# Forty more zero products on the tensor engine, and row sums in four buffers, in an attention and two-MLP kernel

## The chip, the cores and the metric

The kernel runs on one core of a Trainium2 chip. The metric is the device time of one execution in microseconds (us). Before the change three timed executions took 489.66, 491.88 and 491.96 us, a median of 491.88 us.

## What is computed

Two batches, eight heads, 768 positions, 64 columns a head, all in float32. The attention is banded: a position sees itself, the 95 before it and 8 global ones, with a bias by distance. Two mixing layers follow it. Cut to what matters:

```
scores = scale * q @ k.T + bias;  scores = where(keep, scores, -1e9)
a = exp(scores - max(scores));  a = a / (sum(a) + 1e-9);  x = a @ v
u = x + (relu(x.T @ w_tok1) @ w_tok2).T
x = u + relu(u @ w_ch1) @ w_ch2
h = relu(x @ w_in);  u, v = halves of h;  v = (v - mean) / sqrt(var + 1e-6)
out = (u * (w_spatial @ v + b_spatial)) @ w_out
```

## The kernel before

**Stages.** The first 110 us or so hold attention; the rest is dense products, where each float32 product is made of three (lines 333 to 335, `mm3`: high by high, low by high, high by low part). Attention is cut into 12 groups of two units for two heads each. For a group TensorE makes the scores (line 461), VectorE adds the bias and takes the row's extreme into `nm` (486), ScalarE takes exp in place in tile `e` with the row sums into `rs` (490), TensorE transposes `e` (496), ScalarE copies the result to `pt` (338), TensorE multiplies with v (522) and transposes back (532), and VectorE divides by the row sums (541, 542, 547). Beside it ScalarE and VectorE turn 64-bit weights into two float32 parts (379 to 386, the staging tile `raw` of pool `stgp`), and TensorE makes the first token products of a half batch (lines 333 to 335, `p<-xh,wth`, in PSUM banks 6 and 7) and the second ones (711 and `p<-wth,hh`).

**What sets the order.** Every step is an `Op` with a list of engines it may run on and an estimated cost. `Plan.run` is a list scheduler: at each step it takes, of the operations that could start first by its estimates, the one with the longest chain of work behind it, and appends its instructions to their engine's queue. The order in each engine's queue is therefore fixed when the program is built. On the chip an engine does its queue in order and waits for semaphores.

**Zero products.** `banded_part` adds `IDLE[0]` products of a tile of zeros into PSUM bank 7 (line 566, 256 columns, bf16), of which nothing is read. The i-th may not be placed before 4.0 + 0.2 i us of the planner's time. Each waits only for the one before it; the first user of bank 7 after them is the second half (f = 1) of the first token products, so all of them stand before that. They are placed where the planner has no other work for TensorE that could start as early, or where their chain is longer than that of the work that could.

**Row sums.** `rs` is a tile of 32 bytes a partition with 3 rotating buffers, in pool `att`, which is filled from one end of SBUF. In the built program `raw`, `bias0`, `bias1` and `e` of that pool begin 32 bytes past a multiple of 64 (`raw` at 172,448), while `pt`, `ct` and `xp`, and the tile `first` that serves as the first `raw`, begin at multiples of 64. The two `raw` buffers of `stgp` are 4,128 bytes long and begin at 83,776 (a multiple of 64) and 87,904 (32 past one).

Of the kernel before, what the change touches and what calls it, by code (L numbers as in the profile page):

```python
# [6 lines left out]
F32 = mybir.dt.float32  # L7
# [9 lines left out]
P = 128  # L17
# [26 lines left out]
RB, OB = (2, 3), (0, 1, 4, 5, 6, 7)  # L44

WARM = 9
IDLE = 40, 4.0, 0.2

SWITCH, TURN = 0.16, 2.0
_OUTS = [((B, S, DM), "float32")]  # L50
# [36 lines left out]
class Plan:  # L87
# [13 lines left out]
    def op(self, where, fn, reads=(), writes=(), pri=None, mode="full"):  # L101
        o = Op(where, fn, self.pri if pri is None else pri, len(self.ops))
        o.mode = mode if where[0][0] == "PE" else None
        o.plan, o.lam = self, self.lam
        for key in reads:
            w, r = self.seen.setdefault(key, [[], []])
            o.deps.update(w)
            r.append(o)
            if isinstance(key[0], Buf):
                key[0].users.append(o)  # L110
        for key in writes:
            w, r = self.seen.setdefault(key, [[], []])
            o.deps.update(r)
            o.deps.update(w)
            self.seen[key] = [[o], []]
            if isinstance(key[0], Buf):
                key[0].users.append(o)
                if key[0].first is None:
                    key[0].first = o
        o.deps.discard(o)  # L120
        self.ops.append(o)
        return o
# [64 lines left out]
def act(n, extra=0.0):  # L187
    return ("ACT", n / 1200 + 0.07 + extra)


def dve(n, x=1):
    return ("DVE", n * 0.00104 / x + 0.07)
# [10 lines left out]
def mm(n, count):  # L203
    return ("PE", count * (max(n, 64) / 2400 + 0.003))
# [70 lines left out]
class Arm:  # L275
# [227 lines left out]
    def group(self, units):  # L503

        op, T, V = self.plan.op, self.T, self.V
        banks = self.scores(units)
        rs = self.buf("att", "rs", [P, 2, 2, 2, 1], F32, 3)  # L510
        pts = [[self.unit(b, 2 * hp + i, u, banks[k][i], rs, k) for i in range(2)] for k, (b, hp, u) in enumerate(units)]
        c = self.bank("c", CB)

        def pv(e):
            for k, (b, hp, u) in enumerate(units):
                v = self.raws[b, hp]()[:, QK:].rearrange("p (t h x) -> p t h x", h=2, x=D)
                for t, o, w in self.tiles(u):
                    blocks = [(o, t)] if t == 0 else [(o, NT + t - 1), (o + P, t)]
                    sl = slice((2 * k + t % 2) * P, (2 * k + t % 2 + 1) * P)
                    for z, (o1, i) in enumerate(blocks):  # L520
                        for h in range(2):
                            T.matmul(c()[h * D:h * D + D, sl], lhsT=v[:, i, h], rhs=pts[k][h]()[:, o1:o1 + P],  # L522
                                     start=(z == 0), stop=(z == len(blocks) - 1))

        op([("PE", sum(3 if u == 0 else 4 for _, _, u in units) * 0.22)], pv,
           [(p,) for x in pts for p in x] + [self.rawk[b, hp] or ("raw0", "v") for b, hp, _ in units], [(c,)], mode="columns")
        ct = self.buf("att", "ct", [P, 512], F32, 1)
        op([act(512), dve(512)], lambda e: self.copy(e, ct(), c()), [(c,)], [(ct,)])

        def back(e):  # L530
            for j in range(4):
                T.transpose(c()[:, j * P:(j + 1) * P], ct()[:, j * P:(j + 1) * P], self.ident)  # L532

        op([("PE", 0.44)], back, [(ct,)], [(c,)])
        for b, hp, u in units:
            if u == 0:
                self.x_at(b, hp)
                if hp % 2 == 0:
                    self.x_alloc(b, hp // 2)
        rks = [(rs, k, j, i) for k in range(2) for j in range(2) for i in range(2)]  # L540
        op([("DVE", 0.08)], lambda e: V.tensor_scalar(out=rs(), in0=rs(), scalar1=1e-9, scalar2=None, op0=ALU.add), [], rks)
        op([("DVE", 0.11)], lambda e: V.reciprocal(rs(), rs()), [], rks)
        for k0, k1 in ((0, 2),) if units[0][1] == units[1][1] else ((0, 1), (1, 2)):
            b, hp, u = units[k0]
            xp, ks = self.xp[b, hp]
            n = 2 * (k1 - k0)
            op([dve(2 * n * D)], lambda e, xp=xp, u=u, n=n, k0=k0, k1=k1: V.tensor_tensor(
                out=xp()[:, 2 * u:2 * u + n].rearrange("p t (h d) -> p t h d", d=D),
                in0=c()[:, 256 * k0:256 * k1].rearrange("p (t h d) -> p t h d", h=2, d=D),
                in1=rs()[:, k0:k1].rearrange("p k t h o -> p (k t) h o").to_broadcast([P, n, 2, D]), op=ALU.mult),  # L550
                [(c,)] + rks, ks[u:u + k1 - k0] + ([("raw0", x) for x in "abv"] if (b, hp) == (0, 1) else []))
        for b, hp, u in units:
            if u == 2:
                self.plan.pri = XP
                self.x_done(b, hp)
                self.plan.pri = 0.0

    def banded_part(self):
# [5 lines left out]
        idle = self.bank("p7", (7,))  # L564
        for i in range(IDLE[0]):
            o = plan.op([mm(256, 1)], lambda e: self.T.matmul(  # L566
                idle()[:, :256], lhsT=self.zero, rhs=self.zero[:, 0:1].broadcast_to([P, 256]), start=True, stop=True), [], [(idle,)], 9.0)
            o.ready = IDLE[1] + i * IDLE[2]
        self.bias = {}
# [428 lines left out]
```

## Time and profile before

| | |
|---|---|
| median of three timed executions | 491.88 us (489.66 to 491.96) |
| the profiled execution | 489.34 us, span 487.6 us |
| PE busy | 479.2 us (98%) |
| DVE, ACT, POOL busy | 295.9, 215.7, 43.9 us |
| zero products | 40, the last one begins at 32.3 us |

PE stands for TensorE, DVE for VectorE, ACT for ScalarE, POOL for GpSimd, SP for the queue that issues the DMAs. Times are from the span's start. A matmul's end is modelled and overlaps the next one, so a short wait of PE hides inside its busy time: it is read from the start of one group of matmuls to the start of the next, or from a group that is longer than the same group elsewhere.

### The profile page before, as it was taken

Reading aid. Unit: us, or ns where it says so; the run is one execution under the profiler, and the core shown is the slowest. Engines: PE = TensorE matmul, PEld = TensorE weight load, DVE = VectorE, ACT = ScalarE, POOL = GpSimd, SP = SyncE. Lnnn points to the kernel's source line nnn. Section 1 sums busy time; section 2 is a strip of 40 time slices with the busy share of each in tenths; the row PEclk is TensorE's granted clock in tenths of the full one; section 3 lists DMA queues with packets and bytes.
Section 4 is the critical chain, followed back from the end, with each engine's and each line's share of the span. In section 5 each row is a group of like instructions: output and inputs, shape, how many; then the busy total and the mean of one; then the engine's idle time right before and its main releaser. Section 6 shows DMA issues by size and latency. Waiting matters only on the chain.

```text
span 487.6 us, 7897 instructions
## 1 busy us (share of the span) xinstructions
PE 479.2 (98%) x3037; PEld 418.9 (86%) x3037; DVE 295.9 (61%) x747; ACT 215.7 (44%) x518; POOL 43.9 (9%) x36
## 2 busy tenths in 40 slices
PE   9999999999999999999989999999999999999996
PEld 5778678989998888888878888988899988899985
DVE  5779988998988986202888772335861511721520
ACT  5999998995655454211233321103422112421111
POOL 0131311111000000000500000003330000000000
PEclk9999999999999999999999999999999999999999
DMA  7645637222343434000023421110000011000012
GB/s 286 248 169 165 253 91 271 104 84 101 123 144 118 165 105 156 0 1 0 1 86 100 153 72 32 40 59 0 1 1 1 0 65 66 1 2 0 1 43 93
DMA packets 10989, 41.48 MB, mean 85 GB/s; under 512 B 1344, under 2 KB 1856, under 8 KB 10048
## 3 DMA queue, kind: packets, MB, share of 16 engines
q1 hardware_dynamic: 10944, 40.90, 23.7%
q8 instruction: 26, 0.43, 0.4%
q14 instruction: 19, 0.16, 0.1%
HBM read 37.75 MB, written 3.15 MB: 84 GB/s over the span
## 4 chain that ended last, share of the span: by engine, by line
PE 87%; DVE 9%; ACT 1%; issue 1%; POOL 1%; DVEq 0%; POOLq 0%; ACTq 0%
PE p L333 24%; PE p L335 24%; PE p L334 24%; PE p L461 4%; PE p L496 3%; PE p L522 3%; DVE first L344 2%; DVE e L486 1%; DVE uy0l L344 1%; PE p L566 1%; PE p L532 1%; PE dummy L248 1%; PE p L711 1%; DVE a L386 1%; DVE raw L344 1%
## 5 line engine op out<-in xcount | busy, mean ns | idle before, releaser
L758 ACT ACTIVATE raw<-p 128x512 fp32r<-128x512 f32 (+1 forms) x48 | 23.5, 490 | 96.3 <-PE p L335 89.5
L333 PE MATMUL p<-raw,w 128*128 128x512 f32 (+1 forms) x192 | 64.8, 337 | 0.0
L334 PE MATMUL p<-raw,w 128*128 128x512 f32 (+1 forms) x192 | 64.7, 337 | 0.0
L335 PE MATMUL p<-raw,w 128*128 128x512 f32 (+1 forms) x192 | 64.6, 336 | 0.0
L490 ACT ACTIVATE e<-e,nm 128x256 f32<-128x256 f32 (+1 forms) x96 | 46.2, 485 | 3.5 <-DVE nm L486 3.5
L759 DVE SCALAR_TENSOR_TENSOR raw<-p,raw 128x512 fp32r<-128x512 f32 (+1 forms) x48 | 26.1, 554 | 35.6 <-ACT raw L758 35.5
L333 PE MATMUL p<-uy1h,w 128*128 128x512 f32 (+2 forms) x128 | 43.2, 337 | 1.2 <-DVE raw L759 1.2
L333 PE MATMUL p<-uy0h,w 128*128 128x512 f32 (+2 forms) x128 | 43.2, 337 | 0.0
L335 PE MATMUL p<-uy1h,w 128*128 128x512 f32 (+2 forms) x128 | 43.2, 337 | 0.0
L335 PE MATMUL p<-uy0h,w 128*128 128x512 f32 (+2 forms) x128 | 43.2, 337 | 0.0
L334 PE MATMUL p<-uy0l,w 128*128 128x512 f32 (+2 forms) x128 | 43.1, 337 | 0.0
L334 PE MATMUL p<-uy1l,w 128*128 128x512 f32 (+2 forms) x128 | 43.1, 337 | 0.0
L379 ACT ACTIVATE c<-raw 128x512 bf16<-128x512 bf16 x42 | 28.3, 675 | 26.6 <-DMA raw<-in_w_in 16.0
L335 PEld LDWEIGHTS p<-raw,w 128*128 128x128 f32 x192 | 36.1, 188 | 4.2
L333 PEld LDWEIGHTS p<-raw,w 128*128 128x128 f32 x192 | 36.1, 188 | 4.0
L334 PEld LDWEIGHTS p<-raw,w 128*128 128x128 f32 x192 | 36.1, 188 | 3.9
L486 DVE CUSTOM_DVE_ANT_0 e<-p,bias 128x256 f32<-128x256 f32 (+1 forms) x96 | 32.8, 396 | 3.3 <-PE p L461 3.1
L344 DVE TENSOR_TENSOR c<-p,bsp 128x384 f32<-128x384 f32 x16 | 8.9, 558 | 39.7 <-PE p L335 39.7
L386 DVE SCALAR_TENSOR_TENSOR a<-raw,q 128x512 f32<-128x512 uint32 x42 | 30.1, 717 | 0.5
L344 DVE TENSOR_TENSOR a<-a,c 128x512 f32<-128x512 f32 x42 | 29.7, 706 | 0.5
L496 PE MATMUL p<-ident,e 128*128 128x128 f32 x176 | 27.1, 280 | 1.0 <-ACT pt L338 1.0
L380 ACT ACTIVATE c<-raw 128x512 bf16<-128x512 bf16 x42 | 28.0, 667 | 0.0
(159 smaller groups left out, 1107.2 us busy)
## 6 DMA issues: line engine op xcount, KB each, us to landing
raw<-in_wch SPq DMA_DIRECT2D x24, 512.0 KB, 3.6
raw<-in_qkv SPq DMA_DIRECT2D x7, 1552.0 KB, 7.2
raw<-in_w_in SPq DMA_DIRECT2D x8, 512.0 KB, 3.8
raw<-in_wt SPq DMA_DIRECT2D x6, 512.0 KB, 3.9
out<-a SPq DMA_DIRECT2D x11, 256.0 KB, 2.0
raw<-in_w_sp SPq DMA_DIRECT2D x6, 384.0 KB, 2.9
raw<-in_w_out SPq DMA_DIRECT2D x4, 512.0 KB, 3.9
first<-in_qkv SPq DMA_DIRECT2D x1, 704.0 KB, 6.3
```

What stands on the lines that cost most here:

```text
L333: T.matmul(o, lhsT=w[0], rhs=x[0], start=first, stop=False)
L334: T.matmul(o, lhsT=w[0], rhs=x[1], start=False, stop=False)
L335: T.matmul(o, lhsT=w[1], rhs=x[0], start=False, stop=last)
L344: self.eng[e].tensor_tensor(out=o, in0=a, in1=b, op=op)
L379: op([act(n)], lambda e: self.SC.mul(pw(), top(), 2.0 ** -112), [(w,)], [(c, 0)])
L380: op([act(n)], lambda e: self.SC.activation(sg(), top(), AF.Sign), [(w,)], [(c, 1)])
L386: op([dve(n)], lambda e: V.scalar_tensor_tensor(out=aa(), in0=mid(), scalar=2.0 ** -36, in1=qq(), op0=ALU.mult, op1=ALU.mult), [(w,), (q,) ...
L486: op([dve(w)], lambda e, j=j, o=o, w=w, bs=bs: V.tensor_tensor_reduce(out=e_()[:, o:o + w], in0=s()[:, o:o + w], in1=bias()[:, bs], scale= ...
L490: op([act(w, 0.2)], lambda e, j=j, o=o, w=w: SC.activation(e_()[:, o:o + w], e_()[:, o:o + w], AF.Exp, bias=nm()[:, j:j + 1], scale=-1.0, ...
L496: T.transpose(m()[:, j * P:(j + 1) * P], e_()[:, j * P:(j + 1) * P], self.ident)
L758: op([act(n)], lambda e, m=m, r=r, sl=sl, n=n: SC.activation(r()[:, 0, sl], m()[:, :n], AF.Relu), [(m,)], [(r, z, 0)])
L759: op([dve(n)], lambda e, m=m, r=r, sl=sl, n=n: V.scalar_tensor_tensor(out=r()[:, 1, sl], in0=m()[:, :n], scalar=0.0, in1=f32(r()[:, 0, sl] ...
```

## The change

`IDLE` becomes 80, so that 40 more zero products are placed, the last not before 4.0 + 0.2 x 79 = 19.8 us of the planner's time. `rs` gets a fourth buffer: that alone moves no instruction, but moves `raw`, `bias0`, `bias1` and `e` of pool `att` by 32 bytes to multiples of 64 (`raw` to 172,416).

```diff
-IDLE = 40, 4.0, 0.2
+IDLE = 80, 4.0, 0.2
...
-        rs = self.buf("att", "rs", [P, 2, 2, 2, 1], F32, 3)
+        rs = self.buf("att", "rs", [P, 2, 2, 2, 1], F32, 4)
```

All engines' queues are the same up to the operations at about 33 us. The counts of all instructions stay the same but for the zero products and one cast of a token weight (`wth<-a`), which goes from ACT to DVE. Behind row 922 of PE's 5,128 (in the channel products of batch 0) the order is the same again.

On PE, just behind the place where the 40 zero products of before have run out, the rows before are these (587 and so on are buffers; L496 transposes `e`, L333 to L335 are token products):

```order
L532 MATMUL p_516<-ident,ct 128x128 x4
L496 MATMUL p_587<-ident,e 128x128 x4
L496 MATMUL p_597<-ident,e 128x128 x4
L522 MATMUL p_604<-pt,raw 64x128 x14
L496 MATMUL p_627<-ident,e 128x128 x4
L333 MATMUL p_638<-xh,wth 128x256
L334 MATMUL p_638<-xl,wth 128x256
L335 MATMUL p_638<-xh,wtl 128x256
...
L461 MATMUL p_656<-raw 128x128
```

After the change the same place reads as follows, with runs of zero products cut to their first:

```order
L532 MATMUL p_516<-ident,ct 128x128 x4
L496 MATMUL p_587<-ident,e 128x128 x4
L566 LDWEIGHTS zero
L566 MATMUL p_157<-zero 128x256
...
L496 MATMUL p_602<-ident,e 128x128 x4
L522 MATMUL p_609<-pt,raw 64x128 x14
L496 MATMUL p_632<-ident,e 128x128 x4
L566 LDWEIGHTS zero
L566 MATMUL p_157<-zero 128x256
...
L461 MATMUL p_654<-raw 128x128
```

Five zero products now stand between two transposes, and seven in the place of the first nine token products. In all, 39 zero products (runs of 5, 7, 6, 1, 5, 8, 5 and 2) now stand in a stretch that held 24 token products, up to just behind the second transpose back (L532) after this place; the last one stands behind the first three token products.

One group further on, PE's rows before are scores, transposes and products with v alone:

```order
L522 MATMUL p_837<-pt,raw 64x128 x16
L461 MATMUL p_868<-raw 128x128
...
L532 MATMUL p_837<-ident,ct 128x128 x4
L461 MATMUL p_899<-raw 128x256
...
L496 MATMUL p_911<-ident,e 128x128 x3
L496 MATMUL p_919<-ident,e 128x128 x3
L461 MATMUL p_929<-raw 128x256
...
L496 MATMUL p_943<-ident,e 128x128 x4
L496 MATMUL p_965<-ident,e 128x128 x4
```

After the change the same rows have token products between them:

```order
L522 MATMUL p_850<-pt,raw 64x128 x16
...
L532 MATMUL p_850<-ident,ct 128x128 x4
L333 MATMUL p_832<-xh,wth 128x256
...
L461 MATMUL p_915<-raw 128x256
...
L496 MATMUL p_933<-ident,e 128x128 x3
L333 MATMUL p_840<-xh,wth 128x256
...
L496 MATMUL p_965<-ident,e 128x128 x4
L333 MATMUL p_840<-xh,wth 128x256
...
L496 MATMUL p_988<-ident,e 128x128 x4
```

As many token products as made room for the zero products, 24, are now spread over this stretch in eight threes.

On ACT, at about 42 us, the rows before are (the accumulator reads behind each exp are not shown as rows of their own):

```order
L490 ACTIVATE e,rs<-e,nm 128x256
L338 COPY pt<-p_696 128x384
L490 ACTIVATE e,rs<-e,nm 128x256
L338 COPY pt<-p_703 128x384
L490 ACTIVATE e,rs<-e,nm 128x256 x7
```

After the change they are:

```order
L490 ACTIVATE e,rs<-e,nm 128x256
L379 ACTIVATE c<-raw 128x512
L338 COPY pt<-p_700 128x384
L338 COPY pt<-p_708 128x384
L490 ACTIVATE e,rs<-e,nm 128x256 x7
```

The first step on the fourth piece of the token weights (L379), which stood some 7 us later, is now ahead of two copies to `pt`.

## Rows read from the trace of the kernel before

**Rows 1.** The page: span, busy time of each engine, chain that ended last

```profile
span 487.6 us, 7897 instructions
...
PE 479.2 (98%) x3037; PEld 418.9 (86%) x3037; DVE 295.9 (61%) x747; ACT 215.7 (44%) x518; POOL 43.9 (9%) x36
...
PE 87%; DVE 9%; ACT 1%; issue 1%; POOL 1%; DVEq 0%; POOLq 0%; ACTq 0%
```

**Rows 2.** Windows: length, busy us of each engine (instructions), TensorE's granted clock, DMA

```profile
33.00:50.00 17.00, 16.75 (x158) 14.02 (x157) 13.49 (x46) 16.20 (x48) 3.16 (x3) 1.00 0.62 226
50.00:70.00 20.00, 18.78 (x161) 13.95 (x160) 19.75 (x73) 19.40 (x60) 5.27 (x5) 1.00 0.47 171
```

**Rows 3.** Timeline of PE, 5 to 33 us: start, length, what, [idle before]

```profile
5.13 0.80 PE L566 MATMUL p<-zero 128*128 128x256 bf16 x3
...
7.21 1.50 PE L566 MATMUL p<-zero 128*128 128x256 bf16 x12
8.64 1.14 PE L461 MATMUL p<-first 64*128 64x256 f32 x8
...
17.65 1.13 PE L461 MATMUL p<-raw 64*128 64x256 f32 x8
```

**Rows 4.** Timeline of PE, 33 to 70 us

```profile
33.49 0.60 PE L496 MATMUL p<-ident,e 128*128 128x128 f32 x4
34.34 0.66 PE L496 MATMUL p<-ident,e 128*128 128x128 f32 x4 [0.25 <-ACT pt L338]
...
40.06 1.57 PE L461 MATMUL p<-raw 64*128 64x256 f32 x8
...
42.53 1.54 PE L461 MATMUL p<-raw 64*128 64x256 f32 x8
...
46.54 0.36 PE L333 MATMUL p<-xh,wth 128*128 128x256 f32 x1
...
47.70 1.04 PE L496 MATMUL p<-ident,e 128*128 128x128 f32 x8
...
56.35 1.65 PE L461 MATMUL p<-raw 64*128 64x256 f32 x8
58.06 0.66 PE L496 MATMUL p<-ident,e 128*128 128x128 f32 x4
59.42 0.65 PE L496 MATMUL p<-ident,e 128*128 128x128 f32 x4 [0.70 <-ACT pt L338]
...
66.24 0.70 PE L461 MATMUL p<-raw 64*128 64x256 f32 x2
67.25 1.13 PE L461 MATMUL p<-raw 64*128 64x256 f32 x6 [0.31 <-DVE nm L486]
```

**Rows 5.** ACT by line and shape: count, busy us, mean ns, idle before

```profile
L490 ACT ACTIVATE e<-e,nm 128x256 f32<-128x256 f32 x80 | 39.9, 502 | 0.6 <-DVE nm L486 0.6
...
L338 ACT COPY pt<-p 128x512 f32<-128x512 f32 x32 | 17.8, 581 | 0.0
...
L338 ACT COPY pt<-p 128x384 f32<-128x384 f32 x15 | 6.9, 468 | 0.8 <-PE p L496 0.7
...
L490 ACT ACTIVATE e<-e,nm 128x128 f32<-128x128 f32 x16 | 6.4, 399 | 2.9 <-DVE nm L486 2.9
```

**Rows 6.** Timeline of ACT at 42 us

```profile
41.93 0.19 ACT L490 ACTIVATION_READ_ACCUMULATOR e<-e,nm 128x1 f32 x1
```

**Rows 7.** Timeline of SP at 39 us (two issues merged)

```profile
38.83 3.78 SPq L378 DMA_DIRECT2D raw<-in_wt  x2
```

**Rows 8.** The page's DMA issues: count, size, median us to landing

```profile
raw<-in_wt SPq DMA_DIRECT2D x6, 512.0 KB, 3.9
```

**Rows 9.** Timeline of DVE, 50 to 60 us

```profile
51.56 0.69 DVE L386 SCALAR_TENSOR_TENSOR a<-raw,q 128x512 f32<-128x512 uint32 x1
...
57.42 1.68 DVE L386 SCALAR_TENSOR_TENSOR a<-raw,q 128x512 f32<-128x512 uint32 x1
```

**Rows 10.** Timeline of POOL at 57 us

```profile
56.73 1.82 POOL L344 TENSOR_TENSOR xl<-first,xh 128x768 fp32r<-128x768 f32 x1 [1.66 <-ACT xh L338]
```

## The prediction

> **What bounds the kernel now.** I read the page first. PE is busy for 479.2 of 487.6 us, and the chain that ended last is PE for 87% [rows 1]. The reader is to see that almost nothing is left to hide behind: what is added to PE's queue comes out at the end, unless it stands where PE waits. So I looked next for where PE waits. The windows of the attention stage, behind the last zero product of before, show PE idle for 0.25 us between 33 and 50 and for 1.22 us between 50 and 70, while ACT is busy for 16.20 of 17 and 19.40 of 20 us and DVE for 19.75 of the second 20 [rows 2]. In that stretch attention goes at the pace of ACT and DVE, and PE has spare time that it fills with token products. The granted clock is 1.00, the level of 2.4 GHz, in both windows.
>
> Idle time in a window is not all of the wait, because the modelled end of a matmul covers up to some 0.2 us of it. The timeline shows the rest. A run of eight score products on 256 columns takes 1.13 to 1.14 us where nothing holds it [rows 3]. At 40.06, 42.53 and 56.35 it takes 1.57, 1.54 and 1.65 us [rows 4]: 0.44, 0.41 and 0.52 us of waiting for a bank. The run at 66.24 ends at 67.25 + 1.13 = 68.38, 2.14 us after its start, so 1.01 us too late [rows 4]. Eight transposes take 1.04 us [rows 4], four about 0.5; the four at 33.49 and at 58.06 are followed by the next four only after 0.85 and 1.36 us [rows 4], which is 0.35 and 0.86 us of waiting for ScalarE's copies.
>
> **The row sums.** The fourth buffer moves no instruction. It moves `raw`, the two biases and `e` from 32 bytes past a multiple of 64 to such a multiple. For PE's reads the trace holds both cases: scores from `first`, at a multiple of 64, take 1.14 us for eight, and from `raw`, 32 past one, 1.13 us [rows 3]. For ACT, exp in `e` takes 399 ns on 128 columns and 502 on 256, 103 ns for 128 more; the copy to `pt`, which is at a multiple already, takes 468 on 384 and 581 on 512, 113 ns for 128 more [rows 5]. So the misplaced tile costs nothing per column. A fixed cost for it could be hidden in an exp; the two slopes differ by 10 ns, and 10 ns either way for 96 exps is 1.0 us of ACT, of which PE would see a part. I take zero, the middle, and keep 0.5 us on both sides.
>
> **The zero products: price.** Twelve of them at 7.21 are followed by the next run at 8.64 [rows 3]: 1.43 / 12 = 0.119 us each. Forty more are 4.77 us of PE. Neither DMA nor ACT nor DVE has work from them.
>
> **What they displace, first place (33 to 49 us).** 39 of them, 4.65 us, stand where 24 token products stood. Nine of those take from 46.54 to 47.70 [rows 4], so 24 take 3.09 us. The waits there that zero products can stand in are 0.35 + 0.44 + 0.41 = 1.20 us. 3.09 + 1.20 = 4.29, so 4.65 us nearly fit and push the rest by 0.36 us. The attention work behind them is held by ACT and DVE, so a push of that size is partly taken up by the next wait.
>
> **Second place (53 to 65 us).** The 24 token products come back here, in threes between scores and transposes, just where PE waited for 0.52 + 0.86 = 1.38 us with nothing else in its queue. Three more come a group later, before the run at 66.24 with its 1.01 us; they take 0.39 us of that wait at most, and I count 0.33. What does not fit is paid: the sum of both places is 4.77 - 1.20 - 1.38 - 0.33 = +1.86 us. Nothing is late next at the second token products, since they started in before long after the first ones had ended: at this point DVE and ACT have still to turn the last weights.
>
> **The wait that the new order adds.** On ACT the step on the fourth piece of token weights now comes right behind an accumulator read that ends at 41.93 + 0.19 = 42.12 [rows 6]. Its DMA is issued at 38.83 [rows 7] and such a transfer lands after 3.9 us [rows 8], at 42.7. That is about 0.6 us of ACT waiting, and two copies to `pt`, seven exps, and on PE the product with v, are queued behind it. PE has six zero products to do meanwhile (0.71 us), and the same step costs nothing when it no longer comes later, where it stood; from nothing to 0.6 us, and I take 0.2. Against this stands one cast of a token weight that leaves ACT for DVE, and the many small lengthenings of PE's runs that I have not counted as waits, which also can take up zero products. I take +1.5 us for the whole.
>
> **Bounds.** From above: no wait is taken up, 4.77 + 0.6 + 0.5 = +5.9 us. From below: all waits listed vanish, 1.20 + 1.38 + 1.01 = 3.59, and the idle time of both windows with them, 0.25 + 1.22 [rows 2], part of which is the same time: 4.77 - 5.06 - 0.5 = -0.8 us.
>
> **An unknown of the same size.** The same VectorE step takes 0.69 us at 51.56 and 1.68 us at 57.42 [rows 9], where a subtraction of POOL runs from 56.73 to 58.55 [rows 10]. The new order moves VectorE's steps against POOL's, so such a stretch of 1.0 us can vanish or arise. The Trainium skill, page "SBUF — State Buffer", section "SBUF: two separate sides", says that GpSimd and some VectorE steps take a shared pair of ports as an exclusive lock for a whole instruction; the trace agrees with it, 1.68 against 0.69 us. One such meeting more on DVE, near its limit from 50 to 70 us, is up to +1.0 us, one less -1.0 us.
>
> **The base.** The trace is of an execution of 489.34 us, 2.54 below the median of 491.88. The four executions known lie at 489.34, 489.66, 491.88 and 491.96, and nothing in the order up to 33 us, which is the same, says which the changed kernel will draw. I put the sum on their mean, 490.71, and get 490.7 + 1.5 = 492.2 us. On the profiled one alone it would be 490.8, on the median 493.4.
>
> **Rivals.**
> - Slower: the zero products take up no wait. PE's waits are set by ACT and DVE; if the push of the first place reaches `pt` and `nm` before these engines are done with their backlog, ACT itself starves and the whole stage slips by what was added. For it: ACT waited for only 0.8 us of 17 and 0.6 of 20 us, so it has no reserve. Against it: an engine that is full is not delayed by a PE that still delivers in time, and the first place fits within 0.36 us. Price 4.77 + 0.6 = 5.4 us: 496.1. It decides when less than half of the waits vanish. Chance 0.22.
> - The waits of the second place close altogether, and those at 66.24 too: the lower bound without the alignment, about -0.3 us: 490.4 us. For it: eight threes are spread over just these runs. Chance 0.2.
> - The clock: the zero products are there to keep PE running. In the trace three of them take 0.80 us at 5.13 and twelve 1.50 us at 7.21 [rows 3]: near 0.24 us against 0.12 each, the two levels of 1.2 and 2.4 GHz; the first stands near the start of all PE work. From 33 to 70 us the clock is granted in full with 40 of them, and PE's longest wait is 0.70 us [rows 2, 4]. So here the added ones save nothing. But if the executions at 491.9 lost their 2.4 us to a fall of the clock in this stretch (4.8 us at half the pace), the added ones would take that away: 489.5 + 1.5 = 491.0 us, and with closed waits 489.2. Chance 0.16. The Trainium skill, page "TensorE: Matmul & The Clock Gate", section "Part 1: The HAM clock gate", has the slow clock as the default that activity lifts; by it this case is possible, and no row here shows it.
> - The change of addresses alone gives the time and the products nothing; it has no chance of its own beyond the 0.5 us above.
>
> **How the numbers follow.** My forecast, +1.5 us, has 0.42, with its own range of +0 to +3 us. I call a difference of over 0.5% (2.46 us) one that a measurement of this kernel can tell from none. Against 491.88 this is below 489.4 or above 494.3. Faster needs closed waits together with the lower executions or with a saved clock: 0.19. Slower is the first rival and the upper end of the forecast on the upper executions: 0.24. The rest, 0.57, is no difference. The range is from 488.9 (closed waits on the lower executions) to 495.6 (short of the first rival in full).
>
> **What would show it.** Right: PE's busy time up by about 4 us with the span up by 1 to 2; line 566 with 80 products, the last near 50 us; the token products between scores and transposes from 53 to 65 us, and runs of eight scores there near 1.13 us; exp at 502 and scores at 1.13 us as before. Wrong: the exps of the last group of attention later by 4 us or more (first rival), or no later at all (second); a granted clock under 1.00 between 33 and 70 us in before's kind of execution; exps or bias steps shorter by more than 10 ns, which would give the addresses a share.

## The result, and the profile after

The changed kernel takes 494.58 us (median of 6, 494.25 to 495.37), the kernel before 491.97 us in the same comparison (489.66 to 493.52): ratio 1.0051, 95% interval 1.0028 to 1.0074. The forecast was 492.2 us, in a range of 488.9 to 495.6, with "within 0.5%" as the likeliest case. By the forecast's own mark for a slowdown (above 494.3 us) the kernel is 0.3 us on the slow side. How large the difference is depends on the executions of before that it is held against: the experiments ran the kernel before many more times, and 87 executions lie between 489.44 and 496.09 us with a median of 493.19, while all six of after lie within 1.2 us. Four executions far outside (three of before, of 585 to 669 us, and one of the second experiment, of 1213 us) are left out. Why the one kernel scatters and the other doesn't is half of the story.

The page of after, as in [rows 1]:

```profile
span 492.5 us, 7980 instructions
...
PE 482.5 (98%) x3077; PEld 421.4 (86%) x3077; DVE 299.9 (61%) x748; ACT 214.4 (44%) x517; POOL 44.4 (9%) x36
...
PE 77%; DVE 10%; ACT 5%; DMA 4%; issue 2%; POOL 1%; SPq 1%; ACTq 0%; DVEq 0%; POOLq 0%
```

PE works 3.3 us more than in [rows 1], the span is 4.9 us longer, DVE works 4.0 us more with one cast more to do, and in the chain that ended last PE has 77% where it had 87: ACT went from 1% to 5, and DMA, which had no part, has 4%. The windows, as in [rows 2]:

```profile
33.00:50.00 17.00, 16.66 (x165) 13.56 (x164) 13.42 (x45) 15.60 (x47) 3.16 (x3) 1.00 0.62 226
50.00:70.00 20.00, 19.74 (x180) 15.55 (x177) 19.50 (x62) 17.16 (x52) 5.23 (x4) 1.00 0.48 169
```

From 50 to 70 us PE is now almost full (19.74 of 20, it was 18.78), as it should be when token products fill its waits. But ACT, which was nearly full with 19.40, now works only 17.16: it starves. The timeline of PE, as in [rows 4]:

```profile
33.89 0.72 PE L566 MATMUL p<-zero 128*128 128x256 bf16 x5
...
40.12 1.48 PE L461 MATMUL p<-raw 64*128 64x256 f32 x8
...
43.05 1.13 PE L461 MATMUL p<-raw 64*128 64x256 f32 x8
...
48.11 0.66 PE L496 MATMUL p<-ident,e 128*128 128x128 f32 x4 [0.34 <-ACT pt L338]
...
58.96 1.13 PE L461 MATMUL p<-raw 64*128 64x256 f32 x8
60.02 0.66 PE L496 MATMUL p<-ident,e 128*128 128x128 f32 x4
...
61.33 0.66 PE L496 MATMUL p<-ident,e 128*128 128x128 f32 x4
...
62.63 0.93 PE L461 MATMUL p<-raw 64*128 64x128 f32 x8
```

The zeros stand where the waits were: the run of eight scores that took 1.54 us takes 1.13, the one of 1.65 is 1.13 at 58.96, and the transposes at 60.02 and 61.33 show no wait where 0.70 us stood. Why ACT starves is told by its own timeline and by those of DVE and POOL around 54 us:

```profile
42.73 0.67 ACT L379 ACTIVATE c<-raw 128x512 bf16<-128x512 bf16 x1 [0.66 <-DMA raw<-in_wt]
...
53.96 0.59 ACT L338 COPY ct<-p 128x512 f32<-128x512 f32 x1 [1.07 <-PE p L522]
...
55.97 0.40 ACT L490 ACTIVATE e<-e,nm 128x128 f32<-128x128 f32 x1 [1.42 <-DVE nm L486]
```

```profile
53.48 1.91 DVE L384 TENSOR_SCALAR q<-c 128x512 int16<-128x512 int16 x1
...
55.65 0.28 DVE L486 CUSTOM_DVE_ANT_0 e<-p,bias 128x128 f32<-128x128 f32 x1
```

```profile
52.97 2.27 POOL L344 TENSOR_TENSOR xl<-first,xh 128x768 fp32r<-128x768 f32 x1 [6.13 <-ACT xh L338]
```

At 42.73 stands the wait for the weights' DMA that was predicted (0.66 us). The big one is new: a step of line 384 that has a mean of 290 ns elsewhere takes 1.91 us, until the subtraction on POOL has ended at 55.24. The row extremes of line 486 come behind it, and the exp behind these waits 1.42 us. For the addresses, exp as in [rows 5]:

```profile
L490 ACT ACTIVATE e<-e,nm 128x256 f32<-128x256 f32 x80 | 39.9, 505 | 2.8 <-DVE nm L486 2.8
```

505 ns at the new address, 502 at the old: no gain.

### The profile page after: what moved, and what is told of

Its sections match the earlier page's. It is cut to its first block, busy times and chain, and to the rows that moved or that the text cites. A ratio compares the mean times of both kernels' runs of the same rounds, so it can differ in the third digit from the quotient of the medians.

```text
span 492.5 us, 7980 instructions
## 1 busy us (share of the span) xinstructions
PE 482.5 (98%) x3077; PEld 421.4 (86%) x3077; DVE 299.9 (61%) x748; ACT 214.4 (44%) x517; POOL 44.4 (9%) x36
## 4 chain that ended last, share of the span: by engine, by line
PE 77%; DVE 10%; ACT 5%; DMA 4%; issue 2%; POOL 1%; SPq 1%; ACTq 0%; DVEq 0%; POOLq 0%
PE p L333 23%; PE p L335 22%; PE p L334 22%; PE p L461 3%; PE p L496 2%; ACT e L490 2%; PE p L522 2%; DMA raw<-in_wch 2%; DVE first L344 2%; DMA ident<-in_ident 1%; ACT pt L338 1%; DVE uy0l L344 1%; DVE a L386 1%; PE p L711 1%; DMA raw<-in_wt 1%
## 5 line engine op out<-in xcount | busy, mean ns | idle before, releaser
L333 PE MATMUL p<-raw,w 128*128 128x512 f32 (+1 forms) x192 | 64.8, 338 | 0.0
L335 PE MATMUL p<-raw,w 128*128 128x512 f32 (+1 forms) x192 | 64.6, 336 | 0.0
L333 PE MATMUL p<-uy1h,w 128*128 128x512 f32 (+2 forms) x128 | 43.2, 337 | 1.2 <-DVE raw L759 1.2
L333 PE MATMUL p<-uy0h,w 128*128 128x512 f32 (+2 forms) x128 | 43.3, 338 | 0.8 <-DVE raw L759 0.8
L335 PE MATMUL p<-uy1h,w 128*128 128x512 f32 (+2 forms) x128 | 43.2, 337 | 0.0
L335 PE MATMUL p<-uy0h,w 128*128 128x512 f32 (+2 forms) x128 | 43.1, 337 | 0.0
L379 ACT ACTIVATE c<-raw 128x512 bf16<-128x512 bf16 x42 | 28.3, 674 | 27.5 <-DMA raw<-in_w_in 15.4
L335 PEld LDWEIGHTS p<-raw,w 128*128 128x128 f32 x192 | 36.1, 188 | 4.2
L333 PEld LDWEIGHTS p<-raw,w 128*128 128x128 f32 x192 | 36.1, 188 | 4.1
L344 DVE TENSOR_TENSOR w<-a,w 128x512 fp32r<-128x512 f32 x36 | 27.8, 772 | 2.2 <-ACT w L338 2.1
```

The source lines that it names most:

```text
L333: T.matmul(o, lhsT=w[0], rhs=x[0], start=first, stop=False)
L335: T.matmul(o, lhsT=w[1], rhs=x[0], start=False, stop=last)
L344: self.eng[e].tensor_tensor(out=o, in0=a, in1=b, op=op)
L379: op([act(n)], lambda e: self.SC.mul(pw(), top(), 2.0 ** -112), [(w,)], [(c, 0)])
```

## The experiments

Four theories. "Price": the 40 products' time comes out at the end. "Order": not their time, but the order that they force costs, by a DMA wait of ACT and a step of DVE that runs into a subtraction of POOL. "Addresses": the fourth buffer matters. And "before scatters": it loses time in most executions to something that the profiled one didn't meet. The first four kernels ran on one chip, the next four on a second, the last three on a third, each time beside the kernel before, whose median was 493.55, 492.73 and 493.24 us there. So a difference of times from two of these groups is uncertain by some 0.5 us.

**The fourth buffer alone.**

```
-        rs = self.buf("att", "rs", [P, 2, 2, 2, 1], F32, 3)
+        rs = self.buf("att", "rs", [P, 2, 2, 2, 1], F32, 4)
```

> The kernel before with the fourth row-sum buffer alone; no instruction moves, only addresses. Theories: (price) the added 2.6 us are TensorE's time for 40 zero products less the waits they fill; (order) they are what the new order does on ScalarE and VectorE: a DMA wait of 0.66 us on ScalarE and a VectorE step that runs into a POOL subtraction, 1.6 us; (addresses) they are the 32 bytes. Price and order expect no difference, 491.5 to 492.5 us on a base of 492.0, exps at 502 ns and eight scores at 1.13 us. Addresses expects 494.6.

492.89 us (490.06 to 494.40, 12 executions), ratio 0.9977 [0.9950, 1.0005]: "addresses" is out, since it wanted 2.6 us more, and the scatter is that of before. Its profile happens to be of a longer execution than the one behind [rows 4], and with the same order on every engine. Up to 59 us the two agree within 0.1 us; then come PE's timeline, its windows, and the landing time of the load of q, k and v (line 427) that was issued at 52.81:

```profile
59.34 0.66 PE L496 MATMUL p<-ident,e 128*128 128x128 f32 x4 [0.70 <-ACT pt L338]
62.73 1.25 PE L461 MATMUL p<-raw 64*128 64x128 f32 x8 [2.73 <-DMA raw<-in_qkv]
63.91 3.04 PE L522 MATMUL p<-pt,raw 128*64 128x128 f32 x28
```

```profile
60.00:63.00 3.00, 0.27 (x5) 0.30 (x6) 2.94 (x12) 3.00 (x10) 1.41 (x2) 1.00 0.61 226
63.00:66.50 3.50, 3.50 (x32) 2.85 (x31) 2.41 (x11) 0.98 (x4) 0.00 (x0) 0.53 0.01 2
```

```profile
raw<-in_qkv SPq DMA_DIRECT2D x1, 1552.0 KB, 9.8
```

PE waits 2.73 us for that load, and then runs 3.4 us at a granted clock near 0.5, the level of 1.2 GHz: 28 products with v take 3.04 us instead of 1.75. In the execution behind [rows 4] the same load (SP's issue, its landing time, and the scores that read it) took 7.2 us and landed at 60.1:

```profile
52.88 0.33 SPq L427 DMA_DIRECT2D raw<-in_qkv  x1
```

```profile
raw<-in_qkv SPq DMA_DIRECT2D x1, 1552.0 KB, 7.2
```

```profile
60.22 0.93 PE L461 MATMUL p<-raw 64*128 64x128 f32 x8
```

No wait, but no reserve either.

**80 zeros alone.**

```
-IDLE = 40, 4.0, 0.2
+IDLE = 80, 4.0, 0.2
```

> The kernel before with 80 zero products alone, row sums in three buffers. Price and order expect the whole of the change, 494 to 495 us. Addresses expects 492.0.

494.39 us (493.79 to 495.35), ratio 1.0016 [0.9991, 1.0042], granted clock 0.999 or more in every execution. This is the time of the whole change (494.58), here 0.8 us above the median of before and not clear of none.

**After's order, without issuing the 40 added zeros** (their products, which nothing reads, are left out).

```
-            o = plan.op([mm(256, 1)], lambda e: self.T.matmul(
+            o = plan.op([mm(256, 1)], lambda e, i=i: i < 40 and self.T.matmul(
```

> The changed kernel with its order on every engine, but the 40 added zero products are planned and not issued. Price expects that their 4.77 us go and the waits that they filled come back: 491.5 to 492.5 us. Order expects the time to stay within 0.8 us of the changed kernel, 493.8 to 495, with the 0.66 us DMA wait of ScalarE at 42 us and the VectorE step of 1.9 us near 53 us still there.

493.92 us (493.66 to 494.41), ratio 1.0012 [0.9988, 1.0037]. So in this order the 4.77 us of products cost 0.5 us; nine tenths stood in waits. "Price" falls, "order" stands. The clock stays at 0.998 or more without them, so in this order they are not what keeps it. Window and DVE, as above:

```profile
33.00:50.00 17.00, 14.26 (x128) 10.30 (x127) 13.41 (x45) 15.62 (x47) 3.17 (x3) 1.00 0.62 222
```

```profile
53.52 1.92 DVE L384 TENSOR_SCALAR q<-c 128x512 int16<-128x512 int16 x1
```

PE is idle for 2.4 us more where the zeros stood, and DVE's long step is there at the same time.

**Before's order with 40 more zeros**, in fives ahead of eight groups of transposes from 33 to 51 us, not in the waits.

```
+            self.turn = getattr(self, "turn", 0) + 1
+            for _ in range(5 if 17 <= self.turn < 25 else 0):
+                T.matmul(m()[:, :256], lhsT=self.zero, rhs=self.zero[:, 0:1].broadcast_to([P, 256]), start=True, stop=True)
```

> The kernel before in its own order, with 40 more zero products in eight fives, each just ahead of four (or three) transposes and into their bank, from 33.5 to 48 us; nothing else moves. Price expects that they cost about what stands in no wait, 2 to 4.8 us: 494 to 496.8. Order expects that TensorE has slack there, because ScalarE and VectorE set the pace: under 1 us, 492.0 to 493.

494.32 us (493.96 to 494.72), ratio 1.0014 [0.9995, 1.0033]. The time alone parts nothing: it lies where "price" expected it (494 to 496.8) and above what "order" gave in us (492.0 to 493), but it is only 0.8 us above the median of before beside it, where "order" had said under 1. The trace tells more. Outside the waits the products delay the transposes back by 3.2 us (48.93 in before, 52.15 here), as the price would have it for two thirds of them; by the next group but one it is 4.7 us (65.33 against 70.06). Between the two stands the same long step, on DVE and on PE (which waits for what follows from it), while POOL's subtraction runs from 56.27:

```profile
56.33 1.91 DVE L384 TENSOR_SCALAR q<-c 128x512 int16<-128x512 int16 x1
```

```profile
59.17 1.13 PE L461 MATMUL p<-raw 64*128 64x256 f32 x6 [1.02 <-DVE nm L486]
```

```profile
56.27 1.82 POOL L344 TENSOR_TENSOR xl<-first,xh 128x768 fp32r<-128x768 f32 x1 [8.68 <-ACT xh L338]
```

Here DVE came 0.06 us after POOL had begun. In before, of which POOL and DVE follow, it comes 0.01 us after and takes 0.29; a step of line 486, amid the same subtraction, takes its usual 0.42:

```profile
53.09 1.97 POOL L344 TENSOR_TENSOR xl<-first,xh 128x768 fp32r<-128x768 f32 x1 [6.42 <-ACT xh L338]
```

```profile
53.10 0.29 DVE L384 TENSOR_SCALAR q<-c 128x512 int16<-128x512 int16 x1
...
53.95 0.42 DVE L486 CUSTOM_DVE_ANT_0 e<-p,bias 128x256 f32<-128x256 f32 x1
```

The expectation of this run had not named the meeting for before's order. From it comes the theory "collision", and from the first run's late load its like for before, which the next four test.

**After, with POOL's subtraction in six pieces** of 128x128 (the order of all engines unchanged).

```
-        self.eng[e].tensor_tensor(out=o, in0=a, in1=b, op=op)
+        [self.eng[e].tensor_tensor(out=o[:, t], in0=a[:, t], in1=b[:, t], op=op)
+         for t in ([slice(i, i + 1) for i in range(NT)] if e == "POOL" and len(o.shape) == 3 else [slice(None)])]
```

> The kernel after, in the same order on every engine; only GpSimd's subtraction x - high part (line 344, 128x768, 1.83 us) is issued as six pieces of 128x128. Theory 'collision': of the 4.5 us that after's order loses, about 2 come from VectorE's step of line 384, which took 1.91 us instead of 0.29 behind that subtraction at 53.5 us and made ScalarE idle for 1.42 us. With pieces it takes at most 0.6 us, the row maxima of line 486 start by 54.4 (55.65 in after), ScalarE's idle time there is under 0.3 us, and the whole takes 492.0 to 493.2 us, with the granted clock at 0.998 or more in all executions. Rival 'order': the later order is slow by itself (ScalarE's DMA wait at 42, the places of the products after 60 us), VectorE's step is hidden; then the step is short and the time stays 494.0 to 495.0 us. Rival 'pieces': a VectorE step behind six pieces waits for all of them, and six take longer than one (2.2 us or more), so L384 stays at 1.9 us or more and the time is 494.4 to 495.2 us.

491.24 us (490.23 to 492.68), ratio 0.9977 [0.9957, 0.9997]: 3.2 us less than the 494.4 of after's order on the other chip, more than expected. DVE, POOL and ACT at the place:

```profile
53.84 0.54 DVE L384 TENSOR_SCALAR q<-c 128x512 int16<-128x512 int16 x1
```

```profile
53.32 3.23 POOL L344 TENSOR_TENSOR xl<-first,xh 128x128 fp32r<-128x128 f32 x6 [6.22 <-ACT xh L338]
```

```profile
55.44 0.40 ACT L490 ACTIVATE e<-e,nm 128x128 f32<-128x128 f32 x1 [0.53 <-DVE nm L486]
```

The six pieces take longer on POOL (3.23 us) and DVE waits for one of them only. Line 486 started at 55.10, not by 54.4, and ACT still waits 0.53 us, so at this place only a part of the gain arises; the rest comes from other held steps (below). A new wait shows, 0.78 us at 63.29 for the load of q, k and v, which took 8.9 us: this order has no reserve for it either once it is faster, and the wider scatter fits that.

**Before, with the same pieces.** The edit is the one above.

> The kernel before, in its own order; only the same subtraction is issued in six pieces. Theory 'late load': most executions of before lose 2 to 4 us because the load of q, k and v (line 427) issued at 52.9 us lands 7.2 to 9.8 us later, where TensorE asks for it at 60.2; the pieces shorten VectorE's steps of line 381 at 35.9 (1.21 to about 0.3 us) and of line 386 at 57.4 (1.68 to about 0.7 us), off the path, and move that load by at most 0.3 us; so executions still scatter, from 489.4 to 494.5 us, with clocks of 0.991 to 1.0 and a median of 492 to 493.8 us. Theory 'collision' for before as well: the step at 57.4 delays the row maxima and the exponentials from which the wait before 59.42 comes; without it the wait of 0.70 us goes, all executions gain about 0.7 us and the clock holds: median 489 to 490 us.

493.10 us (489.34 to 494.01), ratio 1.0003 [0.9984, 1.0023], clock 0.992 to 1.00: the scatter stays, as "late load" said. Its trace holds a trap, PE and DVE:

```profile
62.46 0.93 PE L461 MATMUL p<-raw 64*128 64x128 f32 x8 [2.12 <-DVE wtl L344]
```

```profile
55.56 0.88 DVE L344 TENSOR_TENSOR wtl<-a,wth 128x512 fp32r<-128x512 f32 x1
```

The wait is put down to a step that had ended six microseconds earlier. The load, issued at 52.99 with 9.3 us to landing, came at 62.3; that was it. And the clock did not fall behind it, as the window shows:

```profile
63.00:66.50 3.50, 3.50 (x44) 2.62 (x40) 2.94 (x12) 2.04 (x8) 0.00 (x0) 1.00 0.00 1
```

This execution took 491.12 us, the one with the wait of 2.73 us and the fallen clock 493.70. So a late load costs its wait in both, and the clock in one.

**Before, with two loads on SP changing places**: q, k and v ahead of the weights (512 KB), no other order changed.

```
-op([dma(P * n * 8)], lambda e: self.SY.dma_start(w()..., src...), [], [(w,)], LDP)
+op([dma(P * n * 8)], lambda e: self.later(lambda: self.SY.dma_start(w()..., src...)), [], [(w,)], LDP)
...
-self.plan.op([dma(P * RAW * 4)], lambda e: self.SY.dma_start(r(), self.A["qkv"][b, hp]), ...)
+self.plan.op([dma(P * RAW * 4)], lambda e: self.later(lambda: self.SY.dma_start(r(), self.A["qkv"][b, hp]), True), ...)
...
+    def later(self, load, raw=False):
+        self.loads = getattr(self, "loads", 0) + (not raw)
+        if not raw and self.loads == 6 and self.banded:
+            self.held = load
+            return
+        load()
+        if raw and getattr(self, "held", None):
+            self.held()
+            self.held = None
```

> The kernel before, in its own order on all compute engines; only two neighbouring loads on SP change places: the one of q, k and v (line 427, 1552 KB, issued at 52.88 us) goes out ahead of the weights' (line 378, 512 KB, 52.31 us), whose first reader stands at 60.8 us. Theory 'late load': the load then lands 6.3 to 6.8 us after its issue, at 59.2 to 59.7 us, TensorE doesn't wait for it at 60.2, the granted clock stays 0.998 or more in all executions, and all take 489.4 to 490.9 us (median near 490.0, ratio to before 0.991 to 0.996, 0.99 of after's). Rival 'clock by itself': the clock falls near 63 us because of the small waits between 54 and 60 us, whatever the load does; then most executions still have 0.991 to 0.997 and take 491.7 to 494.5 us. Rival 'late weights': the weights now come too late for ScalarE at 60.8 and the wait only moves: 491 to 493 us with the clock at 1.0.

489.94 us (489.38 to 490.41), ratio 0.9952 [0.9936, 0.9968], clock 0.998 or more throughout: one exchange of two issues removes the scatter and 2.8 us of the median of its comparison (492.73). The DMA issues and PE:

```profile
raw<-in_qkv SPq DMA_DIRECT2D x1, 1552.0 KB, 6.3
raw<-in_wt SPq DMA_DIRECT2D x1, 512.0 KB, 7.2
```

```profile
59.25 0.66 PE L496 MATMUL p<-ident,e 128*128 128x128 f32 x4 [0.70 <-ACT pt L338]
59.84 1.07 PE L461 MATMUL p<-raw 64*128 64x128 f32 x8
```

The load lands after 6.3 us, PE goes on at once, and the weights, now after 7.2 us, are still in time. The wait of 0.70 us is unchanged and the clock holds: PE's small waits from 54 to 60 us do not lower it. This kernel also shows before's side of the collision, DVE and POOL:

```profile
52.93 0.28 DVE L384 TENSOR_SCALAR q<-c 128x512 int16<-128x512 int16 x1
```

```profile
52.93 1.98 POOL L344 TENSOR_TENSOR xl<-first,xh 128x768 fp32r<-128x768 f32 x1 [6.40 <-ACT xh L338]
```

Here the two begin together, DVE takes its 0.28 us, and it is POOL that is longer (1.98 for 1.83).

**Both edits on before.**

> The kernel before with both edits: the load of q, k and v ahead of the weights' load, and GpSimd's subtraction in six pieces. Theory 'late load' with 'collision': no late load and no VectorE step behind GpSimd, 488.8 to 490.3 us in all executions, clock 0.998 or more, between nothing and 1 us faster than the swap alone, since before's collisions at 35.9 and 57.4 us lie off the path or cost at most 0.7 us. Rival 'pieces': the six pieces are longer and delay the token products or the scores: 490.5 to 492 us, slower than the swap alone.

489.10 us (488.85 to 489.52, 6 executions), ratio 0.9939 [0.9919, 0.9960]: as "late load" with "collision" expected, 0.8 us less than the exchange alone, so the longer pieces cost nothing here.

**Both edits on after; the exchange alone on after; both on before again**, these three together on one chip.

> The kernel after (80 zero products, its own order on the compute engines) with both edits: the load of q, k and v ahead of the weights' load, and GpSimd's subtraction in six pieces. What is left between it and the same two edits on before's order (489.1 us) is what 80 zeros and their order cost when neither a late load nor a held VectorE step falls on them. Theory 'two accidents': the load no longer makes TensorE wait (0.78 us at 63.3 with the pieces alone), all executions lie close together, 489.6 to 490.8 us, that is 0.5 to 1.7 us above before with both edits. Rival 'zeros cost': the 40 added products take their 4.8 us less the waits of some 3 us as the forecast reckoned, and ScalarE's wait at 43 us with it: 490.8 to 492.0 us.

> The kernel after with the swap of the two loads alone. In after the load of q, k and v lands at 62.0 us and TensorE asks for it at 62.6, so it waits for nothing there; what after loses is VectorE's held step at 53.5 us. Theory: the swap does nothing, 494.0 to 494.8 us, ratio to after 0.999 to 1.001. Rival: after loses by the late load too, in places that the profiled execution doesn't show: 491.5 to 493.5 us.

> The kernel before with both edits once more (six executions so far, median 489.10 us), beside the two others on the same chip. Expected 488.8 to 489.6 us in all executions, ratio to before 0.992 to 0.996.

490.71 us (490.25 to 491.75), ratio 0.9963 [0.9940, 0.9985]; 494.19 us (493.76 to 496.84), 1.0034 [1.0011, 1.0056]; 489.60 us (489.07 to 490.33), 0.9944 [0.9924, 0.9964]. The exchange does nothing for after, as expected: without it after's load lands at 53.90 + 8.1 = 62.0 us, and PE asks at 62.63. The pieces then give 494.19 - 490.71 = 3.5 us. And 80 zeros with their order, with neither accident, cost 490.71 - 489.60 = 1.1 us, which lies in what "two accidents" expected (0.5 to 1.7) and, at 490.71, just short of what its rival did (490.8): this run hardly parts the two. Three ranges were too narrow: after with both edits reaches 491.75 where 490.8 was to be the end, before with both edits 490.33 where 489.6 was, and one execution of after with the exchange took 496.84 at a clock of 0.997, which nothing here explains. Before with both edits beats before and after.

Where 3.5 us come from, one row of DVE's timeline for each held step of after from 33 to 125 us:

```profile
35.85 1.22 DVE L381 TENSOR_SCALAR c<-c 128x512 int16<-128x512 int16 x1 [0.85 <-ACT c L379]
...
59.33 1.67 DVE L386 SCALAR_TENSOR_TENSOR a<-raw,q 128x512 f32<-128x512 uint32 x1
...
77.66 1.81 DVE L384 TENSOR_SCALAR q<-c 128x512 int16<-128x512 int16 x1
...
91.69 2.20 DVE L344 TENSOR_TENSOR w<-a,w 128x512 fp32r<-128x512 f32 x1
...
114.15 0.99 DVE L381 TENSOR_SCALAR c<-c 128x512 int16<-128x512 int16 x1 [1.00 <-ACT c L379]
...
119.42 2.32 DVE L344 TENSOR_TENSOR w<-a,w 128x512 fp32r<-128x512 f32 x1
```

With the one at 53.48 these are seven; with two more that are 0.2 us over they make 9.3 us over the usual time of their kinds, and each of the nine lies over an instruction of POOL. In the profiled execution of before there are six, 5.2 us; with both edits 3.7 us on after and 3.6 on before. POOL itself works longer with the pieces (55.3 us on after with both edits, 44.5 with the exchange alone), so what they gain comes through DVE. The groups of DVE by line, in after and then in after with both edits, show it in the means:

```profile
L344 DVE TENSOR_TENSOR w<-a,w 128x512 fp32r<-128x512 f32 x36 | 27.8, 772 | 2.2 <-ACT w L338 2.1
...
L384 DVE TENSOR_SCALAR q<-c 128x512 int16<-128x512 int16 x42 | 15.3, 364 | 0.5
```

```profile
L344 DVE TENSOR_TENSOR w<-a,w 128x512 fp32r<-128x512 f32 x36 | 25.1, 698 | 2.2 <-ACT w L338 2.1
...
L384 DVE TENSOR_SCALAR q<-c 128x512 int16<-128x512 int16 x42 | 12.6, 299 | 0.5
```

## Why the prediction came out right, and where its steps did not

The time fell into the range, and that was in good part luck. The difference of 2.6 us passes the 2.46 that the forecast had called "no difference"; against the larger samples of before it is 0.8 us (494.39 against 493.55) and 1.0 (494.19, with the exchange, against 493.24). And a small difference comes out only because two terms that the sum didn't have nearly cancel: meetings of DVE with POOL cost after 3.5 us (494.19 against 490.71) and before 0.8 (489.94 against 489.10), and the late load costs before 2.8 (492.73 against 489.94) and after nothing. With the 1.1 us of the zeros, this makes 1.1 + 3.5 - 0.8 - 2.8 = 1.0 us, near the 0.8 and 1.0 measured. Of the signs named, PE's busy time went up by 3.3 us as forecast (about 4), but the span by 4.9 and not by 1 to 2, and before's order did show a granted clock under 1.00 between 33 and 70 us, which was to be a sign of being wrong.

- **Zeros less waits, +1.86, with the rest +1.5.** Right in kind, 0.4 us too much. Undisturbed, the change costs 1.1 us (490.71 against 489.60). The products themselves cost 0.5 in after's order with its meetings (494.39 against 493.92); what they cost without these was not run. The waits do close as forecast: the runs of 1.54 and 1.65 us fell to 1.13 us.
- **The wait on ACT, estimated at 0.6 us, counted 0.2.** The wait is there, 0.66 us at 42.73. Its cost isn't separated from that of the order.
- **The row sums, nothing.** Right: 0.9977 [0.9950, 1.0005], exp at 505 and 399 ns.
- **The meeting of DVE with POOL, "up to +1.0 us", left out of the sum.** The term that was mis-sized. The price was read from one step (1.68 against 0.69 us, [rows 9, 10]) and one meeting. A step that comes at the wrong moment is held until POOL's instruction has ended, 1.6 us for line 384, there were several, and they added up: the pieces take 3.5 us off after with the exchange and 0.8 off before with it, so the meetings cost the change about 2.7 us. (Across chips, 494.19 - 489.94 - 1.1 would be 3.1.) The rows to foresee it were there: in before line 384 and POOL's subtraction begin 0.01 us apart (53.10 and 53.09), so a shift of 0.05 us could turn that meeting.
- **The base, 490.71 as the mean of four executions.** The step failed. It took the two levels for an unexplained draw that before and after share. After does not share them: of the 87 executions of before, 11 have a granted clock of 0.998 or more and take 489.44 to 490.94 us; the other 76 have less and take 491.35 to 496.09. In both traces of a longer execution of before's order the load of q, k and v is late and PE waits (2.73 and 2.12 us), and in one the clock then falls; that the others lose their time so too is inferred from the exchange, which leaves none of them. The chain of waits of the profiled execution could not show it, since that one (489.34 us, clock 1.00) is of the kind of the 11. The row to foresee it was there too: a load issued at 52.88 that takes 7.2 us, and a reader at 60.22.
- **The rival of the clock.** Half right: the longer executions do lose about what it said (2.4 us; the medians of the 11 and the 76 are 489.83 and 493.29, 3.5 us apart), and in one trace the clock does fall in this stretch. But there the fall has 1.6 us, and the wait ahead of it 2.73. The added zeros are not what prevents it: after holds the clock without them (0.998 or more, the third experiment). What its order changes is the reserve: the load is read 8.73 us after its issue (53.90 to 62.63) where before reads it after 7.34 (52.88 to 60.22), and the fourth experiment, with 8.63 (56.12 to 64.75) in before's order, holds the clock in all its executions too.
- **The first rival (ACT starves).** ACT does starve, 17.16 us of work where it had 19.40, and the last exp of attention begins 3.1 us later than in the profiled execution of before. But it is not the zeros that starve it: without them that exp begins as late (108.86 against 108.79 us), and with both edits at 105.87, against 105.13 in before with both.
- **The second rival, waits closed altogether (-0.3 us).** Not so; 1.1 us is left.

The Trainium skill, page "SBUF — State Buffer", section "SBUF: two separate sides", says more exactly which steps meet: VectorE's in a mode that uses two ports, or with two inputs from SBUF, against GpSimd's; whichever starts first keeps the shared pair for its whole instruction. The rows agree in all three points: held are steps of one int16 tile (1.91 for 0.29) and steps with two SBUF tiles (2.32 for 0.69), not line 486, which reads one tile from PSUM and one from SBUF (0.42 us at 53.95 in before, amid POOL's 53.09 to 55.06), and the step that began with POOL was not held while one 0.06 us later was. By that rule the kinds of step that can be held could have been listed beforehand; which of them would meet, to 0.05 us, could not.

**What stays open.** Why the same load, issued in the same order, takes 7.2 us in one execution and 9.3 or 9.8 in another, and why the clock fell behind one long wait and not behind the other. And the experiments removed the meetings by the pieces only: that a shared pair of ports is what holds DVE rests on the rule and on the rows that agree with it.

## What to carry to other kernels

A kernel that scatters by 1% may have a step with no reserve somewhere, as this one had: look for a transfer whose landing and whose first reader lie within some tenths of a microsecond, in the fastest execution too, and change its place in the queue before anything is tuned on the median. When an order is moved, don't ask only what PE's queue gains; list which VectorE steps will now begin inside a GpSimd instruction, and try to cut that instruction into pieces if it is long. And split the price from the order: the same program without the added work tells in one run which of the two the time is paid for.

## What was not expected of the hardware

Six pieces of a POOL subtraction take 2.67 to 4.62 us in place of 1.82 to 2.29, and are the better choice still, by 3.5 us in after's order and by 0.3 to 0.8 us in before's (489.94 against 489.60 and 489.10). A load of 1552 KB that is issued 0.6 us behind one of 512 KB landed after 7.2 to 9.8 us, and after 6.3 to 7.1 us when it went first; the one of 512 KB then took 7.2 to 7.9 us in place of 3.6 to 4.5. And the cost of a late load can be more than its wait: after 2.73 us of idle PE the granted clock was 0.53 from 63.0 to 66.5 us, which took about 3.5 x (1 - 0.53) = 1.6 us more (an estimate), while after 2.12 us of idle PE it stayed at 1.00.
